# Granule 1's mask as a table multiply, and bias tables scaled per head, in an attention and feed-forward kernel

## The chip, the cores and the metric

The kernel runs on one core of a Trainium2 chip. A core has engines that work side by side, each through its own instructions in order: TensorE (PE in the profile, with PEld for its weight loads), VectorE (DVE), ScalarE (ACT), GpSimd (POOL) and SyncE (SP). They wait for one another through semaphores. Loads from memory are DMA transfers that POOL, SP or ACT issue. The metric is the device time of one execution in microseconds (us); lower is better.

## What is computed

Sliding-window attention with a few global keys and a distance bias, followed by a feed-forward layer with a squared relu. Cut to what matters (B = 4, H = 8, S = 768, D = 64, n_global = 8, n_local = 96, d_ff = 2048):

```python
scores = scale * q @ k.T
rel = pos[:, None] - pos[None, :]
is_global = pos[None, :] < n_global
is_local = (rel >= 0) & (rel < n_local)
keep = is_global | is_local
dist = where(is_global & ~is_local, n_local, abs(rel))
slopes = 2.0 ** (-8.0 * (arange(H) + 1) / H)
scores = where(keep, scores - slopes[:, None, None] * dist, -1e9)
a = softmax(scores)
x = a @ v                           # (B*S, 512)
h = maximum(x @ w_in, 0)            # 512 -> 2048
out = (s * h * h + b) @ w_out       # 2048 -> 512
```

Inputs and output are f32; the kernel works in bf16 with f32 sums. The results of the exps are not reduced by the row's maximum: the kernel divides by the sum that a column of ones in v gives.

## The kernel before

**Granules.** The 4 x 768 rows are worked through as 12 granules j of 256 rows (GB = 2 blocks i of P = 128). Granules 0, 3, 6 and 9 begin a batch (g = 0), the others do not. For a pair of heads hp (of 4) a granule goes through these steps, each a helper that emits its instructions at once, so that the order of the calls is the order on every engine:

- `T_mm`, `T_quads` transpose q and k on TensorE, half the heads in each of two PSUM tiles, and `T_ev` evicts them to kT and qT (granules 0 to 2; later ones are transposed by a DMA that SP issues, `XB`).
- `KO`, `VO` (L333 to L360) copy, for a granule that does not begin a batch, the keys and values of the *other* block that each block needs: the previous 128, with the first NG = 8 replaced by the global ones.
- `S_mm` (L383) computes transposed scores (keys on partitions, queries in columns) into a PSUM tile scA (even hp) or scB (odd hp). A granule that begins a batch has 3 x 128 columns a head, the others 4 x 128: own block for query block 0, other block for 0, other block for 1, own block for 1.
- `S_post` (L403) takes the exp on ACT into a bf16 tile pt.
- The bias and the mask go in by one of two ways. *Biased* (granules 0 and 1): ahead of the scores, `SB_mm` (L373) puts slope x distance (or -30000) into the PSUM tile by a matmul of `diag` (a diagonal with the head's slope, L219) with `base` (distances and mask, five blocks of 128 columns, L180 and L246 to L250), and the scores add to it. *Multiplied* (granules 2 on): `S_mul` (L412) multiplies pt, after the exp, by `tmpl` = exp(slope x base), a table per head that `make_tmpl` (L253) makes on ACT.
- `A` (L423) multiplies by v on TensorE, `A_norm` (L457) divides on DVE into xn, `XT_half`, `XT_pe`, `XT_dma` transpose xn to xT.
- `P1(j, fp)` (L518) is one eighth of the first feed-forward matmul, 8 matmuls of 256 columns into a PSUM tile of tag psh or pso; ACT takes the relu (L538), and the square runs on DVE either by the next `flush` (L514), or later by `Q(j, fp)` (L551) where the call says "late". `P2_mm` (L582) is a quarter of the second matmul for 128 rows, 4 matmuls of 512 columns; from granule 3 on `W_mm` (L676) does that work with fewer products.

**Loads.** POOL issues nearly all loads (L190 to L209) in one fixed order: v of granule 0, k and q of 1, w_in chunks 0 and 1 of 8, v of 1, w_in chunks 2 to 7, k, q, v of granule 2, three quarters of w_out, two scalars, k of granule 3, the last quarter of w_out, q and v of 3, granule 4. `P1(j, fp)` reads w_in chunk fp. POOL's loads use eight completion semaphores in turn, so a load is issued only after the eighth before it has landed. Granule 0's q and k come by SP and ACT. `pace` makes POOL wait for a tile before it issues the next granule's loads; `pace(raw[1, 0])` (L936) stands ahead of granule 5.

**Order around the change** (L813 to L941): granule 0's attention; granule 1's transposes, with granule 0's `A` and `XT_half` between them; granule 1's scores, with the first P1 of granule 0; its `A`; the P1 of granules 0 and 1, in which the tables of `make_tmpl` are spread (two after granule 1's scores, six between L886 and L906); granule 2; the second matmul of granules 0 and 1; the first P1 of granule 2 (L989), and then `period(3)`, whose first instructions are S(3, 0) (scores of granule 3). The steady order of later granules is `steady` (L1026).

**PSUM.** Tags psh (two tiles), pso, av, scA, scB: a call that takes a tile waits until its last user has read it.

Of the kernel before, what the change touches and what calls it, by code (L numbers as in the profile page):

```python
# [8 lines left out]
F32 = mybir.dt.float32  # L9
BF16 = mybir.dt.bfloat16  # L10
# [8 lines left out]
def kernel(  # L19
# [196 lines left out]
        nc.gpsimd.dma_start(b_bc[:], moe_b.to_broadcast((P, 1)))  # L216


    diag = const.tile([P, H, P], BF16, name="diag")  # L219
    def make_diag(h, eng):  # L220
        scale = float(2.0 ** (-8.0 * (h + 1) / H) / QSCALE)
        if eng == "act":
            nc.scalar.activation(diag[:, h, :], ident[:], ACT.Copy, scale=scale)
        else:
            nc.vector.tensor_scalar_mul(diag[:, h, :], ident[:], scale)
# [9 lines left out]
    def idle(n, tag="pso", cols=4 * P):  # L235
        ps = PS[tag].tile([P, 4 * P], F32, name="ps_i", tag=tag)
        for _ in range(n):
# [5 lines left out]
                stop=True,  # L243
            )

    nc.vector.tensor_copy(base[:, 0, :], base[:, 1, :])  # L246
    nc.vector.tensor_scalar_max(base[0:NG, 0, :], base[0:NG, 0, :], -float(NL))
    nc.vector.memset(base[0:NG, 2, :], -float(NL))
    nc.vector.tensor_copy(base[:, 3, :], base[:, 2, :])
    nc.vector.tensor_copy(base[:, 4, :], base[:, 1, :])  # L250
    tmpl = const.tile([P, H, 5 * P], BF16, name="tmpl")

    def make_tmpl(h):  # L253
        slope = float(2.0 ** (-8.0 * (h + 1) / H))
        nc.scalar.activation(
            tmpl[:, h, :], base[:].rearrange("p a c -> p (a c)"), ACT.Exp, scale=slope
        )


    tps = {}  # L260
# [13 lines left out]
                        ident[:],  # L274
                    )

    def T_quads(j, nm, tags=("psh", "psh"), own=False):
        a = 0 if nm == "k" else 1
        for half in range(2):
            if own or (j, half) not in tps:  # L280
                tps[j, half] = PS[tags[half]].tile([P, 2, 2, GT], BF16, name="ps_t", tag=tags[half])
            tps[j, half, nm] = tps[j, half]
        for e in range(2):
            for i in range(4):
                for half in range(2):
                    r = slice(half * D, (half + 1) * D)
                    for hi in range(2):
                        nc.tensor.transpose(
                            tps[j, half][hi * D : (hi + 1) * D, a, e, i * D : (i + 1) * D],
                            nat[nm, j][r, 2 * e + hi, i * D : (i + 1) * D],  # L290
                            ident[r, r],
                        )
# [40 lines left out]
    def KO(j):  # L333
# [11 lines left out]
        )  # L345
        kos[j] = ko

    def VO(j):
# [24 lines left out]
    def SB_mm(j, hp, which=None):  # L373
        ps = sc_tile(j, hp, which)
        n = ncols(j)
        c0 = 0 if n == 3 * P else P
        m = base[:].rearrange("p a c -> p (a c)")[:, c0 : c0 + n]
# [34 lines left out]
    def S_mul(j, hp):  # L412
        n = ncols(j)
        pt = pts[j, hp]
        if True:
            c0 = 0 if n == 3 * P else P
            m = tmpl[:, 2 * hp : 2 * hp + 2, c0 : c0 + n]
            nc.vector.tensor_tensor(pt[:, :, 0:n], pt[:, :, 0:n], m, ALU.mult)  # L418

    def SS(j, hps, which=None):  # L420
        for hp in hps:
# [1 line left out]
        for hp in hps:  # L423
            S_post(j, hp)

    def A(j, hp, tag="av", norm=True):
# [5 lines left out]
        av = PS[tag].tile([P, GB, 2, 65], F32, name="ps_av", tag=tag)  # L432
        for i in range(GB):
            for hi in range(2):
                h = 2 * hp + hi
                if first:
                    ops = [(i, vaug[b % 2][:, i, h, 0:65])]
                    if i == 1:
                        ops.append((2, vaug[b % 2][:, 0, h, 0:65]))
                else:  # L440
                    ops = [
                        ((0, 3)[i], vaug[b % 2][:, g * GB + i, h, 0:65]),
                        ((1, 2)[i], vos[j][:, i, h, 0:65]),
                    ]
                for n_, (c, vv) in enumerate(ops):
                    nc.tensor.matmul(  # L446
# [71 lines left out]
            gs = pend.pop(0)  # L518
            nc.vector.tensor_tensor(gs, gs, gs, ALU.mult)

    def P1(j, fp, sq="dve", tag="psh"):
        if j not in gT:
            gT[j] = gpool.tile([P, FC, GT], BF16, name="gT", tag="gT")
        ps = PS[tag].tile([P, 2, GT], F32, name="ps_1", tag=tag)
# [9 lines left out]
                )  # L534
        gs = gT[j][:, 2 * fp : 2 * fp + 2, :]
        flush()
        if j < W0:
# [349 lines left out]
    P1(0, 6)  # L887
    T_quads(2, "k", ("pso", "av"))
    T_ev(2, 0, "k")
    T_ev(2, 1, "k", "act")  # L890
# [296 lines left out]
```

The softmax here doesn't subtract the row's maximum and nothing guards it: scores larger than these inputs give would overflow.

## Time and profile before

| | |
|---|---|
| median of 4 runs | 209.47 us (208.18 to 210.08) |
| profiled execution | 208.86 us, its span 207.1 us |
| PE, DVE, ACT, POOL busy | 96%, 82%, 57%, 36% of the span |
| P1 matmuls of 256 columns (L528) | 768, 273 ns each |
| exps (L408) | 48, 953 ns in the mean over two shapes |
| S_mul of 128x1024 (L418) | 28, 687 ns |
| tables of make_tmpl (L255) | 8, 738 ns in the median |
| bias matmuls (L379) | 16, eight of 384 and eight of 512 columns |
| loads by POOL: v / w_in / w_out | 8.3 / 8.1 / 10.1 us from issue to landing (median) |

A row of instructions reads: line, engine, operation, out<-in by the program's names, shapes, count, busy time and mean duration, and the idle time of the engine ahead of them with what ended most of it. Matmuls are pipelined, so a matmul's duration (273 ns) is longer than the distance between two (about 110 ns); distances are read from the starts in the timeline. The chain of waits is followed back from the last instruction: at each step to what released it, or to the instruction before it on its engine.

### The profile page before, as it was taken

What the parts mean: (1) busy time and instruction counts of PE and PEld (TensorE: products, weight loads), DVE (VectorE), ACT (ScalarE), POOL (GpSimd) and SP (SyncE); (2) the same over time, 40 slices, a digit from 0 to 9 for tenths busy, and PEclk for the clock granted to TensorE, in tenths of its full rate; (3) what the DMA queues carried; (4) which work ended last, traced back from release to release, by engine and by line L of the source; (5) the groups of instructions that cost most, each with busy time, mean ns of one, the idle gap of its engine ahead of it and who ended that gap; (6) DMA issues with size and microseconds to landing.
All of it is one profiled execution on the core that took longest, in us unless ns stands there. A gap on an engine that the chain in (4) does not pass through costs nothing.

```text
span 207.1 us, 5605 instructions
## 1 busy us (share of the span) xinstructions
PE 199.4 (96%) x2291; PEld 160.9 (78%) x2299; DVE 169.4 (82%) x409; ACT 118.7 (57%) x181; POOL 74.3 (36%) x98
## 2 busy tenths in 40 slices
PE   6999999998899999999999999999999999999993
PEld 2667876546666678888888888988988988988883
DVE  3785576799789989788799799788799799787693
ACT  5779799456788666626536536536546546524400
POOL 8994673854555009108119109119000000000000
PEclk9999999999999999999999999999999999999999
DMA  5999999999999969999999999999965040040022
GB/s 159 196 183 198 190 194 191 174 155 148 91 154 162 131 188 94 173 154 150 198 120 109 198 97 101 195 122 135 199 80 150 31 118 37 0 152 3 2 104 101
DMA packets 103962, 27.64 MB, mean 133 GB/s; under 512 B 91392, under 2 KB 102016, under 8 KB 103936
## 3 DMA queue, kind: packets, MB, share of 16 engines
q0 software_dynamic: 70976, 13.11, 88.3%
q1 hardware_dynamic: 31904, 13.64, 34.8%
q10 hardware_dynamic: 1056, 0.52, 0.9%
q8 instruction: 18, 0.29, 0.6%
q14 instruction: 8, 0.07, 0.2%
HBM read 27.26 MB, written 6.29 MB: 162 GB/s over the span
## 4 chain that ended last, share of the span: by engine, by line
PE 66%; DMA 19%; POOL 6%; DVE 4%; ACT 1%; issue 1%; SPq 0%; POOLq 0%
PE ps L528 30%; PE ps_w L702 15%; PE ps_wb L702 7%; DMA w_in_bf<-in_moe_w_in_dram 5%; DMA qnat<-in_q_dram 5%; DMA w_out_bf<-in_moe_w_out_dram 4%; PE ps_wa L702 4%; DMA qT<-qnat 4%; PE ps_av L446 3%; PE ps_s L395 3%; PE ps L589 3%; POOL w_in_bf L129 2%; POOL vaug L112 2%; DMA xT<-xn 1%; DVE pt L418 1%; DVE o_pr L627 1%
## 5 line engine op out<-in xcount | busy, mean ns | idle before, releaser
L528 PE MATMUL ps<-xT,w_in_bf 128*128 128x256 bf16 x768 | 96.6, 273 | 0.4 <-DVE xn L464 0.2
L528 PEld LDWEIGHTS <-w_in_bf 128*128 128x128 bf16 x768 | 72.7, 98 | 11.1 <-DVE xn L464 0.5
L540 ACT ACTIVATE gT<-ps 128x512 bf16<-128x512 f32 x72 | 43.1, 598 | 58.4 <-PE ps L528 55.9
L408 ACT ACTIVATE pt<-ps_s 128x1024 bf16<-128x1024 f32 (+1 forms) x48 | 43.1, 953 | 2.8 <-PE ps_s L395 2.8
L702 PEld LDWEIGHTS <-sw 128*128 128x128 bf16 x288 | 28.1, 98 | 3.4
L418 DVE TENSOR_TENSOR pt<-pt,tmpl 128x1024 bf16<-128x1024 bf16 (+1 forms) x40 | 25.1, 647 | 3.1 <-ACT pt L408 2.6
L556 DVE TENSOR_TENSOR gT<-gT 128x512 bf16<-128x512 bf16 x68 | 25.8, 416 | 1.8 <-ACT gT L540 1.6
L112 POOL DMA_DIRECT2D vaug<-in_v_dram x24 | 21.5, 910 | 3.3 <-DMA w_out_bf<-in_moe_w_out_dram 1.6
L702 PEld LDWEIGHTS <-gT 128*128 128x128 bf16 x208 | 19.7, 98 | 3.2 <-issue 0.2
L464 DVE TENSOR_TENSOR xn<-ps_av,rc 128x256 bf16<-128x256 f32 x48 | 20.4, 425 | 1.7
L125 POOL COPY pdum<-xT 1x1 bf16<-1x1 bf16 x5 | 3.8, 766 | 48.9 <-DMA xT<-xn 48.9
L589 PE MATMUL ps<-w_out_bf,gT 128*128 128x512 bf16 x74 | 18.8, 379 | 0.4 <-issue 0.2
L702 PE MATMUL ps_w<-tw,sw 128*128 128x256 bf16 x144 | 18.7, 273 | 0.0
L712 DVE SCALAR_TENSOR_TENSOR u<-ps_w,s_bc,bvec 128x256 f32<-128x256 f32 x27 | 12.9, 479 | 6.3 <-PE ps_w L702 6.3
L446 PEld LDWEIGHTS <-pt 128*128 128x128 bf16 x352 | 15.3, 98 | 3.6 <-DVE pt L418 1.2
L104 POOL DMA_DIRECT2D qnat<-in_q_dram x18 | 15.9, 896 | 4.2 <-DMA w_out_bf<-in_moe_w_out_dram 2.4
L104 POOL DMA_DIRECT2D knat<-in_k_dram x18 | 15.9, 890 | 4.0 <-DMA kT<-knat 2.6
L538 ACT ACTIVATE gT<-ps 128x512 bf16<-128x512 f32 x24 | 14.2, 599 | 5.2 <-PE ps L528 5.2
L446 PE MATMUL ps_av<-vaug,pt 128*128 128x65 bf16 x224 | 16.4, 194 | 0.3 <-DVE pt L418 0.2
L463 DVE RECIPROCAL rc<-ps_av 128x4 f32<-128x4 f32 x48 | 8.7, 182 | 9.3 <-PE ps_av L446 9.1
L589 PEld LDWEIGHTS <-gT 128*128 128x128 bf16 x96 | 8.8, 98 | 8.1
L395 PE MATMUL ps_s<-qT,kT 64*128 64x128 bf16 x224 | 12.6, 218 | 1.2 <-DMA qT<-qnat 1.2
(99 smaller groups left out, 239.9 us busy)
## 6 DMA issues: line engine op xcount, KB each, us to landing
out_dram<-o_pr SPq DMA_DIRECT2D x10, 512.0 KB, 6.2
vaug<-in_v_dram POOLq DMA_DIRECT2D x24, 128.0 KB, 8.3
knat<-in_k_dram POOLq DMA_DIRECT2D x22, 128.0 KB, 6.2
qnat<-in_q_dram POOLq DMA_DIRECT2D x22, 128.0 KB, 7.7
w_in_bf<-in_moe_w_in_dram POOLq DMA_DIRECT2D x8, 256.0 KB, 8.1
w_out_bf<-in_moe_w_out_dram POOLq DMA_DIRECT2D x4, 512.0 KB, 10.1
out_dram<-o_pr SPq DMA_DIRECT2D x3, 256.0 KB, 2.6
raw<-in_q_dram ACTq DMA_DIRECT2D x2, 256.0 KB, 4.9
```

The source lines that it names most:

```text
L104: nc.gpsimd.dma_start(t[:, i, :, :], src[b, :, sb * P : (sb + 1) * P, :].rearrange("h p d -> p h d"))
L112: nc.gpsimd.dma_start(vaug[b % 2][:, sb, :, 0:D], v[b, :, sb * P : (sb + 1) * P, :].rearrange("h p d -> p h d"),)
L395: nc.tensor.matmul(ps[:, hi, oc * P : (oc + 1) * P], lhsT=kt[r, :], rhs=qT[j][r, hp, i * P : (i + 1) * P], start=not biased, stop=not bias ...
L408: nc.scalar.activation(pt[:, :, 0:n], ps[:, :, 0:n], ACT.Exp, scale=QSCALE)
L418: nc.vector.tensor_tensor(pt[:, :, 0:n], pt[:, :, 0:n], m, ALU.mult)
L446: nc.tensor.matmul(av[:, i, hi, :], lhsT=pt[:, hi, c * P : (c + 1) * P], rhs=vv, start=n_ == 0, stop=n_ == len(ops) - 1,)
L464: nc.vector.tensor_tensor(xn[j][:, :, 2 * hp : 2 * hp + 2, :], av[:, :, :, 0:D], rc[:].to_broadcast((P, GB, 2, D)), ALU.mult,)
L528: nc.tensor.matmul(ps[:, i, :], lhsT=w_in_bf[:, kc, fc * P : (fc + 1) * P], rhs=xT[j][:, kc, :], start=(kc == 0), stop=(kc == KC - 1),)
L540: nc.scalar.activation(gs.rearrange("p f (r t) -> p f r t", r=2), ps[:].rearrange("p f (t r) -> p f r t", r=2), ACT.Relu,)
L556: nc.vector.tensor_tensor(gs, gs, gs, ALU.mult)
L589: nc.tensor.matmul(po[j, tb], lhsT=gT[j][:, fc, tb * P : (tb + 1) * P], rhs=w_out_bf[:, fc, :], start=(fc == 0), stop=(fc == FC - 1),)
L702: nc.tensor.matmul(wt[j, ps], lhsT=lhs[:, f, :], rhs=rhs[:, f, :], start=first and f == 0, stop=f == HF - 1, skip_group_check=True,)
```

## The change

1. `base` has three blocks of columns in place of five (0: own block of a batch's first block, 1: own block, 2: other block). Per head there is now `bias` = base x slope x 8 in bf16, eight tables of 384 columns (six on DVE, two on ACT), in place of the eight diagonals. `SB_mm`, still used for granule 0, multiplies the identity by `bias`.
2. `tmpl` is exp(bias / 8) and has three blocks per head. It is made by three exps of 1024 elements on ACT: blocks 1 and 2 of heads 0 to 3 early in granule 0, of heads 4 to 7 ahead of granule 1's exps, block 0 of all heads before granule 2's second pair of scores.
3. The columns of a granule that does not begin a batch are now own, other, own, other, so that `S_mul` reads blocks 1 and 2 twice, through a broadcast dimension.
4. Granule 1 is masked by `S_mul`, not by `SB_mm`. Its ko and vo are made in pieces, its q is transposed into scB's tile, its transposed k and q are evicted by other engines, its `S_mul`, `A_norm` and the late squares of granule 0 have new places, one relu runs on DVE, and P1(0, 6) comes ahead of P1(1, 0) to P1(1, 3).

On each engine the loads that POOL issues and what SP issues keep their order; from granule 2's transposes on, the order of the matmuls is as before.

```diff
-    base = const.tile([P, 5, P], BF16, name="base")
+    base = const.tile([P, 3, P], BF16, name="base")
...
-    diag = const.tile([P, H, P], BF16, name="diag")
-    def make_diag(h, eng):
...
-    for h in range(H):
-        make_diag(h, "act" if h >= 4 else "dve")
...
+    nc.vector.memset(base[0:NG, 2, :], -float(NL))
     nc.vector.tensor_copy(base[:, 0, :], base[:, 1, :])
     nc.vector.tensor_scalar_max(base[0:NG, 0, :], base[0:NG, 0, :], -float(NL))
-    nc.vector.memset(base[0:NG, 2, :], -float(NL))
-    nc.vector.tensor_copy(base[:, 3, :], base[:, 2, :])
-    nc.vector.tensor_copy(base[:, 4, :], base[:, 1, :])
-    tmpl = const.tile([P, H, 5 * P], BF16, name="tmpl")
-
-    def make_tmpl(h):
-        slope = float(2.0 ** (-8.0 * (h + 1) / H))
+    bias = const.tile([P, H, 3, P], BF16, name="bias")
+    tmpl = const.tile([P, H, 3, P], BF16, name="tmpl")
+
+    def make_bias(h, eng=None):
+        scale = float(2.0 ** (-8.0 * (h + 1) / H) / QSCALE)
+        if eng == "act":
+            nc.scalar.activation(bias[:, h], base[:], ACT.Copy, scale=scale)
+        else:
+            nc.vector.tensor_scalar_mul(bias[:, h], base[:], scale)
+
+    def make_tmpl(h0, h1, lo, hi):
         nc.scalar.activation(
-            tmpl[:, h, :], base[:].rearrange("p a c -> p (a c)"), ACT.Exp, scale=slope
+            tmpl[:, h0:h1, lo:hi, :], bias[:, h0:h1, lo:hi, :], ACT.Exp, scale=QSCALE
         )
+
+    for h in (0, 4, 1, 5, 2, 3, 6):
+        make_bias(h, "act" if h in (4, 5) else None)
...
+    def KO_own(half):
+        hs = slice(2 * half, 2 * half + 2)
+        nc.vector.tensor_copy(kos[1][:, hs, 1, NG:P], kT[0][:, hs, 2 * P + NG : 3 * P])
+
+    def KO_prev():
+        ko = kos[1] = work.tile([P, HP, GB, P], BF16, name="ko", tag="ko", bufs=2)
+        nc.vector.tensor_copy(ko[:, :, 0, NG:P], kT[0][:, :, P + NG : 2 * P])
+        nc.vector.tensor_copy(
+            ko[:, :, :, 0:NG], kT[0][:, :, 0:NG].unsqueeze(2).to_broadcast((P, HP, GB, NG))
+        )
+
+    def VO_prev():
...
+    def VO_own():
...
     def SB_mm(j, hp, which=None):
...
             nc.tensor.matmul(
-                ps[:, hi, 0:n], lhsT=diag[:, 2 * hp + hi, :], rhs=m, start=True, stop=False
+                ps[:, hi, 0:n],
+                lhsT=ident[:],
+                rhs=bias[:, 2 * hp + hi].rearrange("p a c -> p (a c)"),
+                start=True,
+                stop=False,
             )
...
-            plan = [own[0] + (0,), own[1] + (3,), (ko[:, hp, 0, :], 0, 1), (ko[:, hp, 1, :], 1, 2)]
+            plan = [own[0] + (0,), own[1] + (2,), (ko[:, hp, 0, :], 0, 1), (ko[:, hp, 1, :], 1, 3)]
...
     def S_mul(j, hp):
         n = ncols(j)
         pt = pts[j, hp]
...
+        m = tmpl[:, 2 * hp : 2 * hp + 2, :, :]
+        if n == 3 * P:
+            m = m.rearrange("p h a c -> p h (a c)")
             nc.vector.tensor_tensor(pt[:, :, 0:n], pt[:, :, 0:n], m, ALU.mult)
+        else:
+            m = m[:, :, 1:3, :].rearrange("p h a c -> p h (a c)")
+            x = pt[:].rearrange("p h (i c) -> p h i c", i=GB)
+            nc.vector.tensor_tensor(x, x, m.unsqueeze(2).to_broadcast((P, 2, GB, 2 * P)), ALU.mult)
...
     cast("k", 0, "act")
     cast("q", 0)
+    make_bias(7)
+    make_tmpl(0, 4, 1, 3)
     T_mm(0, 0, "k")
...
     S_post(0, 3, True)
+    KO_prev()
     A(0, 0, "pso")
     A(0, 1)
     T_quads(1, "k")
     T_ev(1, 0, "k", "act")
     A(0, 2, "scA")
-    XT_half(0, 0, "act", "pso")
-    A(0, 3, "scB")
-    T_quads(1, "q")
-    T_ev(1, 1, "k", "act")
-    XT_half(0, 1, "dve", "av")
-    KO(1)
+    A(0, 3, "pso")
+    XT_half(0, 0, "act", "av")
+    KO_own(0)
+    T_quads(1, "q", both="scB")
     T_ev(1, 0, "q", "act")
+    XT_half(0, 1, "dve", "psh")
+    make_tmpl(4, 8, 1, 3)
     T_ev(1, 1, "q")
-    SB_mm(1, 0)
-    P1(0, 0, "dve", "pso")
-    SB_mm(1, 1)
-    S_mm(1, 0, True)
-    S_post(1, 0, True)
-    S_mm(1, 1, True)
-    S_post(1, 1, True)
-    P1(0, 1)
-    SB_mm(1, 2)
-    S_mm(1, 2, True)
-    S_post(1, 2, True)
-    VO(1)
-    SB_mm(1, 3)
-    S_mm(1, 3, True)
-    S_post(1, 3, True)
-    A(1, 0)
-    A(1, 1, "pso")
-    P1(0, 2)
-    make_tmpl(0)
-    make_tmpl(1)
-    A(1, 2)
-    P1(0, 3)
-    A(1, 3, "pso")
+    T_ev(1, 1, "k")
+    KO_own(1)
+    S_mm(1, 0)
+    S_post(1, 0, mul=False)
+    P1(0, 0, "late", "pso")
+    VO_prev()
+    S_mm(1, 1)
+    S_post(1, 1, mul=False)
+    VO_own()
+    S_mul(1, 0)
+    P1(0, 1, "late", relu="dve")
+    S_mm(1, 2)
+    S_post(1, 2, mul=False)
+    S_mul(1, 1)
+    P1(0, 2, "late")
+    S_mm(1, 3)
+    S_post(1, 3, mul=False)
+    A(1, 0, norm=False)
+    A(1, 1, "pso", norm=False)
+    S_mul(1, 2)
+    A_norm(1, 0)
+    P1(0, 3, "late")
+    A_norm(1, 1)
+    S_mul(1, 3)
+    A(1, 2, "scA", norm=False)
+    A_norm(1, 2)
+    P1(0, 4, "late")
+    A(1, 3, "scB", norm=False)
+    A_norm(1, 3)
     XT_half(1, 0, "act", "av")
-    P1(0, 4)
+    Q(0, 0)
+    P1(0, 5, "late")
     XT_half(1, 1, "dve", "pso")
-    P1(0, 5)
+    for f in range(1, 6):
+        Q(0, f)
+    P1(0, 6)
     P1(1, 0)
...
     P1(1, 3)
-    make_tmpl(2)
-    P1(0, 6)
     T_quads(2, "k", ("pso", "av"))
...
-    make_tmpl(3)
     P1(1, 4)
...
-    make_tmpl(4)
     P1(1, 5)
     SS(2, (0, 1))
     P1(1, 6)
     P1(1, 7)
-    make_tmpl(5)
-    make_tmpl(6)
-    make_tmpl(7)
+    make_tmpl(0, 8, 0, 1)
```

More of the change, by code (lines that the diff above doesn't have):

```diff
@@ L216, in load_scalars @@
         nc.gpsimd.dma_start(b_bc[:], moe_b.to_broadcast((P, 1)))
-    diag = const.tile([P, H, P], BF16, name="diag")
-    def make_diag(h, eng):
[L221 to L225, printed above, removed]
-    for h in range(H):
-        make_diag(h, "act" if h >= 4 else "dve")
     for b in range(2):
@@ L275, in T_mm, with T_quads @@
                     )
-    def T_quads(j, nm, tags=("psh", "psh"), own=False):
+    def T_quads(j, nm, tags=("psh", "psh"), own=False, both=None):
         a = 0 if nm == "k" else 1
+        if both:
+            t = PS[both].tile([P, 2, 2, 2, GT], BF16, name="ps_t2", tag=both)
+            for half in range(2):
+                tps[j, half] = t[:, half]
         for half in range(2):
@@ L346, in KO @@
         kos[j] = ko
+    def KO_own(half):
[8 more added lines that the diff above has]
+    def VO_prev():
+        vo = vos[1] = work.tile([P, GB, H, VW], BF16, name="vo", tag="vo", bufs=2)
+        nc.vector.tensor_copy(vo[:, 0, :, 0:65], vaug[0][:, 1, :, 0:65])
+        nc.vector.tensor_copy(vo[0:NG, 0, :, 0:65], vaug[0][0:NG, 0, :, 0:65])
+    def VO_own():
+        vo = vos[1]
+        nc.vector.tensor_copy(vo[:, 1, :, 0:65], vaug[0][:, 2, :, 0:65])
+        nc.vector.tensor_copy(vo[0:NG, 1, :, 0:65], vaug[0][0:NG, 0, :, 0:65])
     def VO(j):
@@ L375, in SB_mm @@
         n = ncols(j)
-        c0 = 0 if n == 3 * P else P
-        m = base[:].rearrange("p a c -> p (a c)")[:, c0 : c0 + n]
         for hi in range(2):
             nc.tensor.matmul(
-                ps[:, hi, 0:n], lhsT=diag[:, 2 * hp + hi, :], rhs=m, start=True, stop=False
+                ps[:, hi, 0:n],
[3 more added lines that the diff above has]
+                stop=False,
             )
@@ L414, in S_mul @@
         pt = pts[j, hp]
-        if True:
-            c0 = 0 if n == 3 * P else P
-            m = tmpl[:, 2 * hp : 2 * hp + 2, c0 : c0 + n]
+        m = tmpl[:, 2 * hp : 2 * hp + 2, :, :]
+        if n == 3 * P:
+            m = m.rearrange("p h a c -> p h (a c)")
             nc.vector.tensor_tensor(pt[:, :, 0:n], pt[:, :, 0:n], m, ALU.mult)
+        else:
+            m = m[:, :, 1:3, :].rearrange("p h a c -> p h (a c)")
+            x = pt[:].rearrange("p h (i c) -> p h i c", i=GB)
+            nc.vector.tensor_tensor(x, x, m.unsqueeze(2).to_broadcast((P, 2, GB, 2 * P)), ALU.mult)
     def SS(j, hps, which=None):
@@ L424, in SS, with A @@
             S_post(j, hp)
-    def A(j, hp, tag="av", norm=True):
+    def A(j, hp, tag="av", norm=True, av=None):
         b, g = bg(j)
@@ L431, in A @@
             xn[j] = xpool.tile([P, GB, H, D], BF16, name="xn", tag="xn", bufs=2)
-        av = PS[tag].tile([P, GB, 2, 65], F32, name="ps_av", tag=tag)
+        if av is None:
+            av = PS[tag].tile([P, GB, 2, 65], F32, name="ps_av", tag=tag)
         for i in range(GB):
@@ L441, in A @@
                     ops = [
-                        ((0, 3)[i], vaug[b % 2][:, g * GB + i, h, 0:65]),
-                        ((1, 2)[i], vos[j][:, i, h, 0:65]),
+                        ((0, 2)[i], vaug[b % 2][:, g * GB + i, h, 0:65]),
+                        ((1, 3)[i], vos[j][:, i, h, 0:65]),
                     ]
@@ L519, in flush, with P1 @@
             nc.vector.tensor_tensor(gs, gs, gs, ALU.mult)
-    def P1(j, fp, sq="dve", tag="psh"):
+    def P1(j, fp, sq="dve", tag="psh", relu="act"):
         if j not in gT:
@@ L536, in P1 @@
         flush()
-        if j < W0:
+        if relu == "dve":
+            nc.vector.tensor_scalar_max(gs, ps[:], 0.0)
+        elif j < W0:
             nc.scalar.activation(gs, ps[:], ACT.Relu)
```

## The prediction

> **What bounds the kernel now.** I read the page first, then the chain of waits from 0 to 80 us, the waits of TensorE between 8 and 60 us, and the timelines of POOL and TensorE.
>
> ```profile
> span 207.1 us, 5605 instructions
> ...
> PE 199.4 (96%) x2291; PEld 160.9 (78%) x2299; DVE 169.4 (82%) x409; ACT 118.7 (57%) x181; POOL 74.3 (36%) x98
> ...
> PEclk9999999999999999999999999999999999999999
> ...
> PE 66%; DMA 19%; POOL 6%; DVE 4%; ACT 1%; issue 1%; SPq 0%; POOLq 0%
> ```
>
> TensorE is busy nearly all the time, but a fifth of the chain is DMA. The chain in order of time says where (start, length, what):
>
> ```profile
> 13.83 10.51 DMA w_in_bf<-in_moe_w_in_dram
> 24.34 0.28 issue
> 24.62 9.21 DMA w_out_bf<-in_moe_w_out_dram
> ...
> 34.12 10.42 DMA qnat<-in_q_dram
> ...
> 44.56 7.56 DMA qT<-qnat
> ...
> 52.16 0.46 PE ps_s L395 x10
> ```
> ```profile
> PE ps_s L395 <- DMA qT<-qnat: 1.2, 1, 1.2
> ```
>
> Up to 52.16 us the path is one stream of loads; TensorE only has to keep up with it. It meets the stream at the scores of granule 3, after waiting 1.2 us. From there to the end it is TensorE's own work: 20.00 of 20 us busy between 100 and 120, the same between 120 and 140, 19.94 between 140 and 160. So this change, all of it ahead of granule 3 except the form of one multiply, gains only if it moves 52.16, and loses only if it eats the 1.2 us first.
>
> The stream also paces the front. POOL issues a load when the eighth before it has landed, 0.28 us later (the "issue" row above). The issues behind w_in chunks 2 to 7 therefore show their landings (start, length, engine, line, issue, idle before):
>
> ```profile
> 17.64 0.61 POOL L92 DMA_DIRECT2D qnat<-in_q_dram  x1 [0.42 <-DMA w_in_bf<-in_moe_w_in_dram]
> 19.03 0.61 POOL L92 DMA_DIRECT2D qnat<-in_q_dram  x1 [0.78 <-DMA w_in_bf<-in_moe_w_in_dram]
> 20.32 0.90 POOL L112 DMA_DIRECT2D vaug<-in_v_dram  x1 [0.68 <-DMA w_in_bf<-in_moe_w_in_dram]
> 21.66 0.88 POOL L112 DMA_DIRECT2D vaug<-in_v_dram  x1 [0.44 <-DMA w_in_bf<-in_moe_w_in_dram]
> 23.25 0.75 POOL L135 DMA_DIRECT2D w_out_bf<-in_moe_w_out_dram  x1 [0.70 <-DMA w_in_bf<-in_moe_w_in_dram]
> ```
> ```profile
> 17.89 1.04 PE L528 MATMUL ps<-xT,w_in_bf 128*128 128x256 bf16 x8
> ...
> 19.01 1.04 PE L528 MATMUL ps<-xT,w_in_bf 128*128 128x256 bf16 x8
> ...
> 20.35 1.04 PE L528 MATMUL ps<-xT,w_in_bf 128*128 128x256 bf16 x8
> ...
> 21.45 5.41 PE L528 MATMUL ps<-xT,w_in_bf 128*128 128x256 bf16 x48
> 26.78 0.45 PE L288 MATMUL ps_t<-ident,knat 64*64 64x64 bf16 x32
> ```
>
> Chunks 2 to 6 land at 17.36, 18.75, 20.04, 21.38, 22.97 (each 0.28 before its row). P1(0,2) to P1(0,5), which read chunks 2 to 5, start at 17.89, 19.01, 20.35, 21.45: already 0.53, 0.26, 0.31, 0.07 us behind their chunks. There is nothing left to gain there.
>
> **The change, part by part.**
>
> *TensorE.* Eight bias matmuls of 512 columns go. Eight 512-column matmuls start at 42.81 and the next group at 44.54, so one costs 0.216 and eight 1.73 us. Granule 0 keeps its eight of 384 columns with another stationary operand: nothing.
>
> *ACT.* Out: 8 tables at 0.738 = 5.9 us, of which five lie between 29.2 and 36.3, and 4 diagonals (0.30 each). In: 2 bias tables of 384 elements, between 0.30 (128 elements) and 0.74 (640), by proportion 0.52; 3 table exps of 1024 elements at 1.07 (0.738 at 640, plus 384 more at the 0.86 ns that separate 640 from 128). The first sits between the cast (ends 5.18) and qT's eviction (5.95, after 0.77 idle). 1.07 against 0.77, less the 0.1 by which neighbours overlap, puts qT some 0.1 to 0.3 later; the scores and exps of granule 0 follow by that much, and it fades at 9.9 us, where granule 1's k is waited for anyway. The second sits ahead of granule 1's first exp (below); without that cover it costs its 1.07.
>
> *DVE.* In: 6 bias tables, between 0.19 (128 elements) and 0.42 (1024), I take 0.26, by proportion; five run before q lands at 4.99, DVE being idle from 3.56 to 5.01. Four multiplies of 1024, 0.69 each = 2.8; one relu out of PSUM at 0.73 (the nearest row, L581); ko and vo in eight pieces instead of four, each between 0.18 (64 elements, L342) and 0.43 (1040, L353), I take 0.3, so 2.3 instead of 1.9.
>
> *Granule 1, walked through.* Transposes of k start at 9.95. Norms of granule 0 leave DVE 0.2 to 0.5 later than now, behind KO_prev, so xT(0) is whole at 13.2 instead of 12.9. qT(1)'s first half leaves ACT at 12.7, S(1,0) runs at 12.8, its exp behind the table exp at 13.8. P1(0,0) runs 13.2 to 14.1; S(1,1) and P1(0,1) end at 15.3, S(1,2) at 15.5. Then P1(0,2) stands at chunk 2, and the 1.73 us that were freed become a wait of about 1.8 us until 17.4. From there TensorE takes P1(0,2), S(1,3), A(1,0), A(1,1), P1(0,3), A(1,2), P1(0,4), A(1,3), P1(0,5) as chunks allow: P1(0,5) at about 21.5 as now. New is that P1(0,6) comes before P1(1,0) to P1(1,3): it cannot start before 23.05, and P1(0,5) is done at 22.4. So 0.6 us is lost: five P1 of 0.88 (the six from 21.45 end at 26.75) end at 27.4, where granule 2's transposes start at 26.78 now. If KO_own(1) also held S(1,0), it would start at 14.7, and S(1,2) end at 17.2: still before chunk 2.
>
> *DVE in that stretch:* from 8.9 to 23.2, 14.3 us, it has 13.2 us by the durations above (8 norms at 0.60, T_ev 2 x 0.69, multiplies 2.8, relu 0.73, two xT and one square at 0.42, the pieces of ko and vo 2.3), and neighbours overlap by some 0.1. The cover: xT(1), needed at 23.9, is ready at about 23.2, so DVE may slip 0.7 before TensorE does.
>
> *From 27.4 to 52.* Granule 2 runs as now, 0.6 late; less ACT work removes part of two waits that are there now (0.41 us at 35.75, 0.34 at 38.41 in TensorE's weight loads), so it is 0.4 late at 42.8 and reaches S(3,0) at 51.1 instead of 50.7. The wait there shrinks from 1.2 to 0.8 us and the end does not move. The step that opens granule 5's loads (46.35) is as late, but its first load waits until 49.34 for a transpose that the stream sets.
>
> *The multiplies of granules 2, 4, 5, 7, 8, 10, 11* (28 of 128x1024) now read one table block twice, a step of zero in a middle dimension. No two-input row has that. Bounds: 0.681 (L674, the same size) to 1.224 (L570, the same size in f32), per multiply -0.01 to +0.54. Nearest is the vo copy with a repeated block (L356), 0.426 against 0.433 for the one without (L353): I take 0. In all +0; at the upper bound see the rivals.
>
> *Two rules that speak against the change.* The nine warm-up matmuls of 512 columns take 3.41 us, although eight take 1.89 later: TensorE starts slow, while the granted clock reads 1.00. Idle times of 1.04 us (before 5.23) and 1.21 (before 52.16) are followed by full pace; the new wait of 1.8 has no row, and would cost at most what one more slow start does, 3.41 less nine times 0.216, 1.5 us, of which 0.8 is still covered: 0 to +0.7, I take 0, its nearest row.
> The Trainium skill, TensorE: Matmul & The Clock Gate, section "The HAM clock gate", puts half pace behind an idle window of about 3.4 us of a free-running clock; by it 1.8 us would leave the sum as it is, and no run here shows a longer idle time.
> The pair of v loads issued at 2.52 took POOL 1.90 us, while two DVE copies beside it took 0.34 and 0.26 against 0.20 for the one before; the pair at 8.39 took 1.79. So DVE and POOL disturb each other by about 0.1, and six bias tables lie beside those first issues: +0.1 to +0.6 on the issues, of which I put +0.1 on the stream, since landing takes 5.1 us for the quickest v load and 10.5 for the slowest of w_in: POOL runs far ahead.
> The Trainium skill, SBUF — State Buffer, section "Who interferes with whom", has a DVE copy or scalar operation in its two-port mode shut POOL out for its whole length; worked out as an estimate, six tables would delay the stream by 1.6 us and give 210.5.
>
> *Sum.* Profiled execution 208.86 (span 207.1, 1.76 around it): -1.73 freed and +1.73 waited for at chunk 2, +0.6 at chunk 6 and -0.6 from the wait at 52.16, +0.1 for POOL: 209.0. The four runs' median, 209.47, lies 0.6 above that execution, so I predict 209.5.
>
> **The rivals.**
>
> *The zero step halves the multiply's pace (slower).* At 1.22 us instead of 0.687, four multiplies add 2.1 us to a granule. Steady granules come every 15.3 us (the P1 at 99.75 and the one at 115.02), in which DVE is busy 88% (70.3 of 80 us between 100 and 180), 13.5. The 15.6 does not fit, and DVE's present idle time (1.8 a granule) would remain in part: 0.3 to 2.1 us for each of seven granules, 2 to 15, say 8: 217. It decides above a multiply of 0.69 + 1.8/4, 1.14. Against it: the vo copy.
>
> *DVE falls behind in granule 1 (slower).* Copies reach 0.61 (ko at 12.80) and 0.83 (vo) beside POOL's issues. Should DVE slip more than 0.7 + 0.8 us, each further us is one at the end; with ten copies at +0.2 it slips 2.0, which gives 210.0, within 1%. Only another 2 us would show.
>
> *The stream is not what holds S(3) (faster).* Were the wait at 52.16 put down to the wrong releaser, the 1.73 us, and no more, could come through: 207.8. Against: the transpose behind it runs 7.6 us, and its load lands 0.02 us before it is issued.
>
> *The change is smaller than it says:* granule 0 keeps its bias matmuls, and only eight go; this is in the sum.
>
> **How the numbers follow.** Within 1% (2.1 us) is about what a measurement here cannot tell from no change; the four runs spread by 1.9. The forecast has 0.68, DVE's slip 0.05, and of the wrong releaser's 0.12 a third, 0.04, lies within 1% too: 0.77. Slower: zero step 0.07, a larger slip or a stream over 2 us late 0.08: 0.15. Faster: 0.08, the wrong releaser with a quick run beside it. The range, 207.4 to 212.0, takes in 207.8, the clock's +0.7, POOL's +0.6 and DVE's 210.0, with the runs' spread around them; it leaves out the zero step.
>
> **What would show it.** TensorE waits some 1.8 us for w_in near 15.5 and 0.5 near 22.5; S(3,0) still waits for the DMA of qT, under 1.2 us, and resumes within 0.3 us of 52.16; the multiplies keep 0.69; from there to the end 155 us. It is wrong if that wait is gone and S(3) starts later, if the multiplies take over 1 us, or if the transposes land before 51.

## The result, and the profile after

The changed kernel takes 210.67 us (median of 44 runs, 208.97 to 214.72) against 209.29 us (63 runs). The ratio is 1.0047, 95% interval 1.0027 to 1.0067, so about 1.0 us slower; this and every ratio below leaves out the runs that lie more than 1.5% above the fastest of their kernel (13 of these 44 and 15 of the 63), so it is smaller than the ratio of the two medians, 1.0066. The profiled execution has a span of 207.8 us against 207.1. In 28 of the 44 runs the mean granted clock was not 1.00 but 0.992 (18 runs, median 210.83) or 0.984 (10 runs, 213.88); the other 16 have a median of 209.67.

The page after, in the lines shown of before:

```profile
span 207.8 us, 5593 instructions
...
PE 198.6 (96%) x2284; PEld 160.3 (77%) x2291; DVE 174.5 (84%) x419; ACT 115.7 (56%) x172; POOL 74.1 (36%) x98
...
PE 66%; DMA 19%; POOL 6%; DVE 4%; ACT 1%; issue 1%; SPq 0%; POOLq 0%
```

TensorE and ACT do less, DVE 5 us more, and the chain's shares are those of before: what bounds the kernel has not changed. The chain up to granule 3's scores (start, length, what), and TensorE's waits from 8 to 60 us:

```profile
13.29 9.97 DMA w_in_bf<-in_moe_w_in_dram
...
24.58 9.11 DMA w_out_bf<-in_moe_w_out_dram
33.69 0.28 issue
33.98 11.36 DMA qnat<-in_q_dram
45.33 0.02 issue
45.35 7.50 DMA qT<-qnat
52.85 0.04 issue
52.90 0.46 PE ps_s L419 x10
```
```profile
PE ps L557 <- DMA w_in_bf<-in_moe_w_in_dram: 1.7, 2, 1.4
PE ps_s L419 <- DMA qT<-qnat: 1.2, 1, 1.2
```

The same stream still ends at the scores of granule 3, but at 52.90 instead of 52.16, and the load of q takes 11.36 us instead of 10.42. From there to the end both profiles need 154.9 us. So the whole difference of the two profiled executions, 0.7 us, lies in the stream. TensorE's own timeline (start, length, line, shapes, idle time before):

```profile
17.51 1.05 PE L557 MATMUL ps<-xT,w_in_bf 128*128 128x256 bf16 x8 [1.41 <-DMA w_in_bf<-in_moe_w_in_dram]
...
23.31 4.54 PE L557 MATMUL ps<-xT,w_in_bf 128*128 128x256 bf16 x40 [0.28 <-DMA w_in_bf<-in_moe_w_in_dram]
27.78 0.45 PE L289 MATMUL ps_t<-ident,knat 64*64 64x64 bf16 x32
...
51.43 0.23 PE L419 MATMUL ps_s<-qT,kT 64*128 64x128 bf16 x2
52.90 0.46 PE L419 MATMUL ps_s<-qT,kT 64*128 64x128 bf16 x10 [1.23 <-DMA qT<-qnat]
```

The freed matmuls became a wait of 1.41 us for w_in chunk 2; P1(0,6) waits 0.28 us for chunk 6; granule 2's transposes start 1.0 us later than before, and TensorE comes to granule 3's scores at 51.43 instead of 50.72. It waits there as long as before, 1.23 us, because the stream has moved by as much. The multiply with the zero step (operation, count, ns shortest/median/longest, first and last start) costs nothing:

```profile
L446 DVE TENSOR_TENSOR pt<-pt,tmpl x32: 668/685/694, 15.9 to 178.9; 128x1024 bf16<-128x1024 bf16 x32
```

Two questions are open: is the later stream the change's doing, and does TensorE's lateness of 0.7 us show in runs where the stream happens to be early?

### The profile page after: what moved, and what is told of

Same layout as the page of the kernel before. It is cut to its first block, busy times and chain, and to the rows that moved or that the text cites. A ratio compares the mean times of both kernels' runs of the same rounds, so it can differ in the third digit from the quotient of the medians.

```text
span 207.8 us, 5593 instructions
## 1 busy us (share of the span) xinstructions
PE 198.6 (96%) x2284; PEld 160.3 (77%) x2291; DVE 174.5 (84%) x419; ACT 115.7 (56%) x172; POOL 74.1 (36%) x98
## 4 chain that ended last, share of the span: by engine, by line
PE 66%; DMA 19%; POOL 6%; DVE 4%; ACT 1%; issue 1%; SPq 0%; POOLq 0%
PE ps L557 30%; PE ps_w L733 15%; PE ps_wb L733 7%; DMA qnat<-in_q_dram 5%; DMA w_in_bf<-in_moe_w_in_dram 5%; DMA w_out_bf<-in_moe_w_out_dram 4%; PE ps_wa L733 4%; DMA qT<-qnat 4%; PE ps_av L475 3%; PE ps_s L419 3%; PE ps L620 3%; POOL w_in_bf L129 2%; POOL vaug L112 2%; DMA xT<-xn 1%; DVE pt L446 1%; DVE o_pr L658 1%
## 5 line engine op out<-in xcount | busy, mean ns | idle before, releaser
L571 ACT ACTIVATE gT<-ps 128x512 bf16<-128x512 f32 x72 | 43.1, 598 | 58.5 <-PE ps L557 56.4
L587 DVE TENSOR_TENSOR gT<-gT 128x512 bf16<-128x512 bf16 x74 | 28.0, 416 | 1.7 <-ACT gT L571 1.6
L446 DVE TENSOR_TENSOR pt<-pt,tmpl 128x1024 bf16<-128x1024 bf16 x32 | 21.3, 685 | 1.9 <-ACT pt L432 1.9
L569 ACT ACTIVATE gT<-ps 128x512 bf16<-128x512 f32 x23 | 13.6, 598 | 8.2 <-PE ps L557 8.2
```

Source lines behind the costliest of these rows:

```text
L446: nc.vector.tensor_tensor(x, x, m.unsqueeze(2).to_broadcast((P, 2, GB, 2 * P)), ALU.mult)
L571: nc.scalar.activation(gs.rearrange("p f (r t) -> p f r t", r=2), ps[:].rearrange("p f (t r) -> p f r t", r=2), ACT.Relu,)
```

## The experiments

Ratios stand to the kernel before, timed beside it on the same chip. "Wait" is TensorE's at granule 3's scores in the profile, "there" when TensorE comes to them. Names with a are edits of the changed kernel, with b of the kernel before.

| run | edit | ratio (95% interval) | there | wait |
|---|---|---|---|---|
| a_again | none | 1.0137 (1.0081 to 1.0193) | 52.33 | 2.00 |
| a_p6back | P1(0,6) back | 1.0075 (1.0043 to 1.0107) | 51.22 | 1.5 |
| b_p6fwd | P1(0,6) forward | 1.0042 (1.0017 to 1.0067) | 51.73 | none |
| b_sp | s, b on SyncE, first | 1.0139 (1.0101 to 1.0178) | 53.42 | none |
| b_again | none | one time, 210.68 | 51.34 | 2.0 |
| b_blate | b later | 0.9938 (0.9906 to 0.9969) | 50.86 | none |
| a_blate | b later | 0.9942 (0.9907 to 0.9977) | 51.32 | none |
| a_pad | 14 short matmuls at the wait | 1.0012 (0.9965 to 1.0058) | 52.59 | none |
| a_warm | 6 long matmuls at the wait | 1.0114 (1.0056 to 1.0171) | 51.96 | 3.09 |
| a_best | b later, granule 1 reordered | 0.9958 (0.9937 to 0.9979) | 51.73 | none |
| a_pad2 | 14 short matmuls at the start | 1.0002 (0.9965 to 1.0038) | 51.13 | 0.56 |
| b_pad2 | the same, before | 1.0003 (0.9964 to 1.0042) | 51.51 | 2.01 |

### The order of P1(0,6), alone

```
 b_p6fwd (before)           a_p6back (changed)
+    P1(0, 6)              -    P1(0, 6)
     P1(1, 0)                   P1(1, 0)
...
     P1(1, 3)                   P1(1, 3)
     make_tmpl(2)          +    P1(0, 6)
-    P1(0, 6)
```

> The changed kernel once more, unedited, for the scatter of the load stream. Theory S (the load stream sets the start of granule 3's scores in every execution, and the change makes the stream itself about 0.7 us later): the last qT transpose of granule 3 lands again near 52.8 us, TensorE waits over 1 us for it, ratio about 1.004. Theory P (the change makes TensorE late and that lateness is what shows): ratio about 1.004 too, with TensorE reaching the scores of granule 3 near 51.4 us. Theory C (the 0.7 us of the first profile is scatter of one execution): the transpose lands anywhere between 51.8 and 53 us, ratio nearer to 1.001.

> The changed kernel with P1(0,6) behind P1(1,0) to P1(1,3) again, as before the change; nothing else. TensorE no longer waits for w_in chunk 6 there (0.28 us), but P1(1,0) may wait up to 0.4 us for the eviction of the second half of xT(1). Theory S: the wait for the qT transpose grows by what TensorE gains, ratio stays at about 1.004. Theory P: the gain of 0.1 to 0.6 us shows, ratio 1.001 to 1.003.

> The kernel before with P1(0,6) ahead of P1(1,0) to P1(1,3); nothing else. P1(0,6) then waits about 0.6 us for w_in chunk 6. Theory S: the 1.2 us wait for qT shrinks by 0.6 us and takes it up, ratio 1.000. Theory P: ratio 1.002 to 1.003.

Putting P1(0,6) back gains 0.2 us of arrival, and the wait grew to 1.5 us, as theory S said. A gain in time is not shown: 1.0075 is above both theories' figures, and its interval meets that of a_again. b_p6fwd missed S's 1.000: the stream was early in its profile (the transpose landed at 51.50), TensorE came at 51.73 and did not wait at all. Its ratio fits theory P. So the 1.2 us that the profile of before shows are not there in every execution; b_again has 2.0 us. The end is set by the later of two arrivals, and the stream's scatters by 2 us: in before, b_again, b_p6fwd and b_pad2, where the order of loads is the same, qT lands between 51.50 and 53.71 us. Most of that comes behind the loads. The last load of granule 3's q lands at 44.20 to 45.15 us in these four, and the transpose behind it needs 7.3 to 9.0 us. The unedited changed kernel, timed again, was 1.0137, not 1.004, and its qT landed at 54.52, not 52.8: ratios of 1.004 and 1.01 are not told apart from one timing to the next.

The loads themselves answer the first question. In the four profiles of the changed kernel with b in its place and no pad of 14 matmuls (after, a_again, a_p6back, a_warm) the last load of granule 3's q lands at 45.33, 45.63, 45.45 and 47.00 us, later than in any of the four above. So the later stream is no scatter of one execution.

### What holds the stream: two loads of 512 bytes

```
 b_sp
-        nc.gpsimd.dma_start(s_bc[:], ...)
-        nc.gpsimd.dma_start(b_bc[:], ...)
+        nc.sync.dma_start(s_bc[:], ...)
+        nc.sync.dma_start(b_bc[:], ...)
...
-    load_scalars()
     more_loads()
...
+    load_scalars()
     idle(9, "av")
```

> The kernel before with the two broadcast loads of s and b (4 bytes to each partition) moved from the middle of POOL's stream of loads to SyncE's queue at the start. In the profile they stand between w_out chunk 2 and granule 3's k and hold the stream from 36.35 to 38.00 us. Theory S: everything behind them lands 1.0 to 1.6 us earlier, the wait for qT vanishes and TensorE starts the scores of granule 3 1.2 us earlier, ratio 0.994 to 0.996. Theory P: TensorE does not wait for the stream in most executions, ratio 0.999 to 1.000.

It missed. The two broadcasts delayed what came behind them at the start as they do in the middle: the first v load took 6.91 us instead of 5.21, w_in chunk 5 landed at 24.10 instead of 21.38, and TensorE was late by itself (53.42). So they were not cheap there either; they have to stand where nothing waits. b is read first at 63.4 us, so it alone was moved behind granule 3's v, in both kernels:

```
 b_blate, a_blate
     def load_scalars():
         nc.gpsimd.dma_start(s_bc[:], ...)
-        nc.gpsimd.dma_start(b_bc[:], ...)
...
         load_v(3)
+        nc.gpsimd.dma_start(b_bc[:], ...)
         load_granule(4)
```

> The kernel before once more, unedited, for the scatter of the stream. Theory S (the change makes the stream later): w_out chunk 2 lands 2.5 us behind chunk 1, as in the three profiles without the change so far, and the qT transpose of granule 3 lands by 52.2 us. Theory C (scatter of single executions): w_out chunk 2 lands up to 3.5 us behind chunk 1 and the transpose near 53 us in this one.

> The kernel before with the broadcast load of b issued behind granule 3's v instead of ahead of its k (s stays). Theory S (the stream sets the start of granule 3's scores): in the profile of before, b keeps three of the 16 DMA engines 1.1 to 1.7 us behind the others; without it granule 3's k and q land about 1 us earlier, the wait for qT falls to 0 to 0.4 us, TensorE starts there at 51.0 to 51.4 us instead of 52.16, ratio 0.995 to 0.997. Theory P (TensorE's own lateness shows, the stream does not): ratio 0.999 to 1.000.

> The changed kernel with the same move of b. Theory S: the qT transpose lands near 51.6 us instead of 52.9, TensorE (there at 51.4) waits 0 to 0.4 us, ratio 0.998 to 1.000, so 1.0 to 1.4 us under the changed kernel. Theory P: ratio stays at 1.004 or above.

SyncE's queue shows the arrival of granule 3's k and q, since a transpose is issued 0.01 to 0.02 us after its load has landed (start, length, line). Before, after, b_blate, a_blate:

```profile
38.88 2.69 SPq L320 DMA_TRANSPOSE kT<-knat  x2
43.17 2.58 SPq L328 DMA_TRANSPOSE qT<-qnat  x2
```
```profile
39.64 3.00 SPq L321 DMA_TRANSPOSE kT<-knat  x2
43.89 2.65 SPq L329 DMA_TRANSPOSE qT<-qnat  x2
```
```profile
37.12 2.71 SPq L320 DMA_TRANSPOSE kT<-knat  x2
41.40 3.19 SPq L328 DMA_TRANSPOSE qT<-qnat  x2
```
```profile
37.02 2.62 SPq L321 DMA_TRANSPOSE kT<-knat  x2
41.22 3.11 SPq L329 DMA_TRANSPOSE qT<-qnat  x2
```

Without b ahead of it, k lands 1.8 us earlier in the kernel before and 2.6 us earlier in the changed one, at the same time in both (0.7 of the 2.6 are w_out chunk 2, ahead of b's old place, which lands at 36.12 instead of 36.83 here). The stream then is no longer the later arrival (chain of a_blate):

```profile
47.89 3.49 PE ps L557 x32
51.39 0.44 PE ps_s L419 x12
51.83 0.16 issue
51.99 1.67 PE ps L620 x7
```

All 12 matmuls of the scores run in one piece. Both kernels gain, 0.6% and, from 1.0047 to 0.9942, 1.0%, more than theory S had forecast (0.995 to 0.997, and 0.998 to 1.000), and they are then equal: medians 208.2 and 208.14, spans 206.2 and 206.3 us. So the loss lies in the stream ahead of granule 3's scores. TensorE comes 0.46 us later in the changed one (51.32 against 50.86), but in b_blate a wait of 0.3 us for a transposed xT near 155 us takes most of that back; the profiles of a_blate, before and after have none there. b_again, the kernel before unedited, has this wait too, so it comes and goes without the change.

Why does a load of 512 bytes take so long? Each load ends with sixteen landing records, one for each DMA engine. They do not name the engine; the last seven of b and of the first part of granule 3's k, in order of time:

```
            10th   11th   12th   13th   14th   15th   16th (us)
before  b  35.67  35.78  35.80  36.18  37.92  37.95  38.00
        k  36.10  36.17  36.23  36.54  38.78  38.78  38.87
after   b  35.57  35.69  38.27  38.50  38.51  38.59  38.77
        k  36.45  36.48  39.09  39.33  39.33  39.45  39.62
a_blate k  35.91  35.93  35.94  36.45  36.72  36.94  37.00
```

Engines that are on time are through with b 0.2 us after s. The late ones are through with b 1.1 to 2.0 us after s (by their places in the order). Three of them are late before, five after.

### Why five instead of three

POOL issues granule 3's v when w_out chunk 2 has landed (idle time before the issue), before and after:

```profile
36.63 1.75 POOL L112 DMA_DIRECT2D vaug<-in_v_dram  x2 [1.64 <-DMA w_out_bf<-in_moe_w_out_dram]
```
```profile
37.11 1.75 POOL L112 DMA_DIRECT2D vaug<-in_v_dram  x2 [2.26 <-DMA w_out_bf<-in_moe_w_out_dram]
```

By granule 2's v the changed kernel's loads land as early as before (28.58 against 28.73 us), and w_out chunk 1 too (33.69, 33.83). Chunk 2 then needs 3.14 us instead of 2.52, on one engine alone: the second latest is through at 36.10. A packet of 16 KB of TensorE's instructions, 0.89 us long, starts at 31.33 in the changed kernel and at 29.62 before, and the earlier ones can be seen in the loads: after the one at 14.17 one engine of sixteen is 0.8 us behind in w_in chunks 2 to 5. Theory F blamed it:

```
 a_pad                                   a_pad2, b_pad2
+    idle(14, cols=16)                  +    idle(14, "av", 16)
     P1(0, 2, "late")                        idle(9, "av")
```

> The changed kernel with 14 matmuls of 16 columns on constants ahead of P1(0,2), inside its 1.4 us wait for w_in chunk 2. They add 28 instructions to TensorE's program and no work that counts. Theory F (the change moves the third 16 KB fetch of TensorE's instructions from 29.6 to 31.3 us, where it delays a DMA engine that is already late, and this is what makes w_out chunk 2 land 0.6 us later): the fetch comes near 29.9 us again, w_out chunk 2 lands 2.5 us behind chunk 1, qT lands near 52.2 us, ratio 1.000 to 1.002. Otherwise: w_out chunk 2 stays 3.1 us or more behind chunk 1, ratio 1.004 or above.

> The changed kernel with 14 matmuls of 16 columns on constants ahead of the warm-up matmuls, 28 more instructions of TensorE before 5 us, where it waits for the first cast anyway. Theory F (the third 16 KB fetch of TensorE's instructions, at 31.3 us in the changed kernel and at 29.6 to 29.9 before, makes w_out chunk 2 late): the fetch comes near 29.8 us, w_out chunk 2 lands 2.5 us behind chunk 1, qT by 52.2 us, ratio 1.001 to 1.003. If the change makes the stream late in another way: w_out chunk 2 3.1 us or more behind chunk 1, qT near 52.9 us, ratio 1.004 or above.

> The kernel before with the same 14 matmuls of 16 columns ahead of the warm-up matmuls, the control of a_pad2. Theory F (the later fetch of TensorE's instructions in the changed kernel is what makes w_out chunk 2 late; there was nothing to mend before): third fetch near 28.4 us, w_out chunk 2 2.5 us behind chunk 1, qT by 52.2 us, ratio 0.999 to 1.001. If the extra instructions help for another reason, in any kernel: ratio 0.995 to 0.997, as a_pad2 stands to the changed kernel.

In both padded kernels chunk 2 needs 2.50 us again, and no loss is left to see (1.0012, 1.0002), though these intervals still meet that of the changed kernel, 1.0027 to 1.0067. Their runs at full clock have medians of 208.77 and 209.21 us, against 208.98 and 209.18 for the kernel before timed beside them. The pad at the start does nothing for the kernel before (1.0003); there chunk 2 needed 2.50 us as forecast, but qT landed at 53.71, not by 52.2, because its transpose took 9.0 us, and the third fetch came at 29.45, not 28.4. Here is POOL's row of a_pad2, to be held against the two above:

```profile
36.53 1.75 POOL L112 DMA_DIRECT2D vaug<-in_v_dram  x2 [1.64 <-DMA w_out_bf<-in_moe_w_out_dram]
```

The fetch of a_pad2 came at 30.16, as forecast, but that of a_pad at 31.43, as late as without a pad, so its time is not what decides. Chunk 2 was late in all four profiles with the change, b in its old place and no pad of 14 (after 3.14, a_again 3.52, a_p6back 3.19, a_warm 3.46 us), and in none of the four without the change whose order of loads is that of before (2.50 to 2.58). So 28 more instructions of TensorE make chunk 2 punctual at both places tried; that their number decides it is not shown, since a_blate, with no instruction of TensorE more, needs 2.53 us with a fetch at 31.20. Which engine serves which fetch, and why b must be queued behind chunk 2 for it to be late, stays open.

The second fetch sorts the runs by another load. In the five profiles in which it starts at 20.98 to 21.22 us (after, a_again, a_p6back, a_blate, a_warm), w_in chunk 6 lands at 23.14 to 23.33 us. In the eight in which it starts at 19.71 to 20.55, chunk 6 lands at 22.70 to 22.96; b_sp, whose loads are all late, is left out. The pads move this fetch from 21.22 to 20.52 and 19.77. That it is also what makes w_out chunk 2 late was not tried.

### The clock

```
 a_warm
+    idle(6)
     P1(0, 2, "late")
```

> The changed kernel with six matmuls of 512 columns on constants ahead of P1(0,2): 1.3 us of work that counts for nothing, inside the 1.4 us wait for w_in chunk 2 that the change made. Theory K (in a part of the executions this wait makes the granted clock fall to one half for 3.41 us right behind it, as the trace of a_again shows from 18.1 and that of a_pad from 18.76 us): TensorE hardly idles there, the clock stays at 1.00 from 18 to 24 us, the slower half of the times (over 210.5 us) thins out, median 208.9 to 209.7, ratio 1.001 to 1.003. What is left over 1.000 is the later stream. Theory S alone (the stream sets the start of granule 3's scores and nothing else matters): median and ratio as the changed kernel, 1.0047. Against both: ratio above 1.006, if the six matmuls hold P1(0,2) up.

Windows of a_again (window, length, busy time of TensorE and its weight loads, DVE, ACT, POOL, granted clock, DMA share, GB/s), then of a_pad, then of b_pad2, which has nothing of the change:

```profile
15.00:18.00 3.00, 1.05 (x16) 0.81 (x16) 2.39 (x6) 1.50 (x2) 1.67 (x3) 1.00 1.48 195
18.00:21.40 3.40, 3.40 (x36) 2.42 (x34) 2.36 (x7) 1.62 (x2) 1.69 (x3) 0.51 1.46 200
21.40:24.00 2.60, 2.60 (x39) 2.37 (x38) 1.51 (x6) 1.67 (x3) 1.45 (x2) 0.98 1.45 192
50.00:55.60 5.60, 3.60 (x37) 2.60 (x36) 4.75 (x8) 4.06 (x8) 5.26 (x6) 1.00 2.73 120
55.60:59.00 3.40, 3.40 (x13) 1.59 (x12) 1.12 (x2) 1.49 (x3) 0.00 (x0) 0.51 1.93 151
```
```profile
18.70:22.10 3.40, 3.40 (x42) 2.72 (x37) 1.72 (x5) 1.86 (x3) 1.82 (x3) 0.51 1.46 198
```
```profile
50.00:54.80 4.80, 2.63 (x30) 1.86 (x28) 3.93 (x7) 3.53 (x7) 3.79 (x5) 1.00 3.18 113
54.80:58.20 3.40, 3.40 (x13) 1.66 (x12) 1.12 (x2) 1.48 (x3) 0.00 (x0) 0.51 1.84 144
```

The clock falls to one half for 3.41 us beside a wait: the fall begins 0.8 to 1.2 us after the wait's end, in a_warm 0.2 us ahead of it. One fall takes 0.008 from the mean clock of a run (3.41 times 0.5 over 208), so 0.992 is one fall and 0.984 two. Of the profiles' waits of 1.6 us and more, five (1.7, 2.0, 2.0, 2.0, 3.1) went with one and three (1.6, 1.8, 2.0) did not; of the shorter ones none did. The two profiles with a fall in granule 1 are among the latest at the scores: a_pad at 52.59 and a_again at 52.33, where a_pad2 came at 51.13. Behind the scores of granule 3 a fall costs its full 1.7 us: b_pad2 goes from 53.75 to granule 3's second scores at 59.77 in 6.0 us, before from 52.16 to 56.49 in 4.3.

a_warm filled the wait for chunk 2, and there the clock stayed at 1.00 in its profile. But the stream was the latest of all, and the fall came at the second wait:

```profile
51.96 0.23 PE L419 MATMUL ps_s<-qT,kT 64*128 64x128 bf16 x2
55.27 0.72 PE L419 MATMUL ps_s<-qT,kT 64*128 64x128 bf16 x10 [3.09 <-DMA qT<-qnat]
```

Its times missed theory K's 208.9 to 209.7 (median 211.52). They do not tell the price of the wait for chunk 2, since the later stream hides it. Other runs say that the wait for qT costs most. a_blate still waits 1.6 us for chunk 2, but not for qT, and 1 of its 12 runs shows a fall. Of the kernel before, whose two profiles have no wait of more than 0.6 us for w_in, 92 runs were timed beside the experiments, on four chips. 29 of them show one fall, and chip by chip their medians lie 2.8 to 3.5 us above those of its runs at full clock.

Falls are also part of three ratios: of the six runs each of a_again, b_sp and a_warm, five, five and three show one or two. Their other runs (210.38, 210.90, median 210.84) lie 0.8% to 1.0% above the full-clock runs of the kernel before timed beside them. The two kernels with b moved do not wait for qT, and their times lie together: 207.40 to 208.55 and 207.96 to 209.28, where the 44 of the changed kernel spread over 5.8 us.

### Both kernels beaten

a_best is a_blate with this as well:

```
+    S_mm(1, 3)
+    S_post(1, 3, mul=False)
+    A(1, 0, norm=False)
     P1(0, 2, "late")
-    S_mm(1, 3)
-    S_post(1, 3, mul=False)
-    A(1, 0, norm=False)
...
-    P1(0, 6)
     P1(1, 0)
...
     P1(1, 3)
+    P1(0, 6)
```

> The changed kernel with three moves: the load of b behind granule 3's v; S(1,3) and A(1,0) ahead of P1(0,2), inside its wait; P1(0,6) behind P1(1,0) to P1(1,3) again. Theory S with TensorE's own path: the qT transpose lands near 50.4 us, TensorE comes to granule 3's scores at 50.6 to 51.0 instead of 51.4, ratio 0.991 to 0.994, under both kernels. Theory K adds: with the wait for chunk 2 cut to about 0.8 us, no execution loses clock there, and the times lie within 1 us of each other. If the moves of granule 1 bring nothing, the ratio is that of b's move alone, 0.994.

Its wait for chunk 2 went to 0.5 us and its times lie within 1 us, as theory K said, but TensorE got new waits of 0.2 to 0.3 us each, for exps, a multiply and xT(1), and came to the scores at 51.73, 0.4 us later than a_blate and not at 50.6 to 51.0. The reordering brought nothing; the gain is the move of one load. b_blate and a_blate, at 0.994, are equal, and a_best is not told apart from them, so the change shows no gain even there.

## Why the prediction was right in its time and wrong in a step

- **The bound.** Right, and shown: up to granule 3's scores the path is the load stream, and a load moved out of it makes both kernels faster, which the removal of 1.73 us of TensorE's work did not. The rival that the releaser was named wrongly falls. It is not so in every execution: in b_p6fwd TensorE came last.
- **The zero step.** Right: 685 ns against 687. The heaviest rival falls.
- **TensorE's front.** Right in kind: the freed 1.73 us became a wait for chunk 2 (1.41 us, forecast 1.8). Sizes were off by 0.3: P1(0,6) starts at 23.31, not 23.05, because chunk 6 landed at 23.27 instead of 22.96; so the transposes start at 27.78, not 27.4, and TensorE arrives at 51.43, not 51.1.
- **DVE and POOL.** Right that it costs next to nothing: the first loads land 0.3 to 0.5 us later, those that POOL does not issue among them (k's first at 4.83 against 4.54), but 0.15 to 0.2 us earlier in a_again, and by granule 2's v they are 0.15 us early. POOL's first two v issues took 1.94 us instead of 1.90, with three DVE tables beside them. What slowed down was DVE: the third of them took 0.62 us, the other two 0.26 and 0.25. The Trainium skill, SBUF — State Buffer, "Who interferes with whom", says that whichever of the two issues first keeps the shared ports for its whole instruction and the other waits; the forecast's estimate of 1.6 us took POOL as the one that waits, which this trace does not show.
- **The step that failed** is the sum's "-0.6 from the wait at 52.16, +0.1 for POOL": the wait did not shrink (1.23 us), since the stream itself came 0.74 us later. It was priced as if only POOL's issuing could move it. In the landing records 0.48 us of the lateness are there when w_out chunk 2 is complete, which one DMA engine holds up, and 0.75 when the first part of granule 3's k is, behind s and b. The forecast's own sign for this, S(3,0) resuming within 0.3 us of 52.16, failed: it resumes at 52.90.
- **The wait of 1.8 us**, taken at 0 with +0.7 as its upper bound, was the wrong end in part of the executions: in the profile after, no fall followed the 1.41 us, but the clock fell behind waits for chunk 2 of 1.7 us (a_pad) and 2.0 (a_again). Over all runs of the changed kernel, those with one fall lie 1.2 us above those at full clock. The Trainium skill, TensorE: Matmul & The Clock Gate, "The HAM clock gate", puts the half clock behind an idle window of about 3.4 us. The length of the half clock agrees (3.41 us); the idle time does not: 1.67 us, half of it, were enough in one execution.
- **The number.** 209.5 forecast, 210.67 measured: the range and "within 1%" held, but they are 4.6 and 4.2 us wide, so that they held says little of the mechanism. The sum lacked about 1 us, the later stream and the falls of the clock that long waits bring. An estimate of their shares: at full clock the changed kernel's 209.67 us lie 0.5 to 0.9 above the kernel before as timed beside the experiments (medians 208.75 to 209.18), near the stream's 0.74; the rest goes with the falls, in 28 of 44 runs against 29 of 92. Two figures do not follow from their own terms: 208.96 and 0.61 make 209.57, and the 210.5 of the two-port rule leaves the 0.61 out.

## What to carry to other kernels

Where a wait ends on a load, look at what is queued ahead of that load, however small: moving 512 bytes gained 0.6%, and removing eight matmuls gained nothing. A slack read from one profile (here 1.2 us) is one draw from a spread of 2 us, and most of the spread came from the transpose behind the loads, so charge a delay that just fits into it with part of its price. And a TensorE wait near 2 us costs more than its length, since half clock may follow it.

## What the hardware showed that was not expected

- A broadcast of 4 bytes to each of 128 partitions held the load stream by 1.2 to 1.8 us (granule 3's k lands at 38.30 to 38.87 us in the four profiles without the change that have it ahead, at 37.10 in b_blate).
- A 16 KB packet of TensorE's instructions takes 0.88 to 0.99 us in the first 41 us, and behind the one at 14.17 us in the profile of before the next loads were 0.8 us late on one of the sixteen DMA engines: w_in chunk 2 was complete on fifteen at 16.58 us and on the last at 17.36. That it is the engine that fetched is inferred from the times.
- The clock fell to one half for 3.41 us beside waits from 1.7 us on, in some executions and not in others (1.75 and 1.98 us without a fall).
